# DeltaNet and a maxout layer on one core: loads asked for in the opening, two masks on GpSimd, inverse copies placed elsewhere, the last output's two stores exchanged

## The chip, the cores and the metric

The kernel runs on one core of one Trainium2 chip. The metric is the device time of one execution in microseconds (us). The engines are named as the profile names them: PE (TensorE, matrix products and transposes), DVE (VectorE), ACT (ScalarE), POOL (GpSimd) and SP (SyncE, which here only issues DMAs). Each engine works through its own list of instructions in order; an instruction that waits holds up everything behind it on its engine. An engine that issues a DMA only starts a transfer; the data land later.

## The reference, cut to what matters

For 4 batches and 8 heads, a state of 48 by 48 is carried along 768 positions, and each position reads it and then corrects it. The result, laid out as 3072 rows of 384, goes through a layer that takes the largest of three products.

```python
k_n = k / (norm(k) + 1e-06)
for t in range(S):
    y[t] = q[t] @ state
    v_old = k_n[t] @ state
    state = state + beta[t] * outer(k_n[t], v[t] - v_old)
x = y.transpose(0, 2, 1, 3).reshape(B * S, H * D)
h = maximum(maximum(x @ w1, x @ w2), x @ w3)
out = h @ w_out
```

w1, w2 and w3 are 384 by 768, w_out is 768 by 384, and all four arrive as 64-bit floats.

## The kernel before, in words

**Chunks.** The 768 positions are cut into 12 chunks of 64 (counter c). Within a chunk the positions depend on each other through a triangular matrix of 64 by 64 per head, which is inverted; then a chunk is a handful of matrix products. Two batches lie side by side on the 128 partitions. Keys and queries are loaded as 24 units (two per chunk), turned on PE (`turn`, line 342, copied out at line 348) and multiplied with each other (`gram`, line 419). A product of keys with keys is called `at`, one of keys with queries `pt`. `pt` must be multiplied with a triangular mask before it is used (`masked`, line 403).

**Inverse.** Chunks are inverted two at a time (`solve`). The first call, `solve(0)`, works on blocks of 16 in 15 steps; each step is one DVE multiplication (line 571, tmp from x_bl and y_bl) and one DVE subtraction (line 575, y_bl from y_bl and tmp), all of it in SBUF. Then the block is transposed (line 583), and its parts are copied by `placed` (line 509) into ut0 (chunk 0) and ut1 (chunk 1), four copies for each. `halves_t`, `halves_z`, `halves_u`, `join_z` and `join_u` join blocks of 16 into 32 and 64: DVE transposes (lines 655 and 657), products p_e (line 695), p_f (706), p_z (723), p_j (736), and copies out of PSUM between them (lines 698, 710, 727, 738). `negated_of` chooses the PSUM tiles and the engines for the copies with changed sign (lines 710 and 738). Then `new` makes p_u (line 781, copied out to u at 786), `to_y` makes p_y (823, copied to y at 827) and `to_x` transposes y into xt (842, 849). The chunks 2 and 3 are inverted by `solve(1)`, whose input comes by way of DRAM: `gram` sends `at` out in stores of 32 KB (line 449, 16 of them on SP), and `blocks(1)` fetches all of it back in another order (line 496, on POOL).

**Weights.** `fetch` (line 224) asks for one of 24 pieces of 384 KB into one of five buffers (w_bits). `weights` turns a piece into 32-bit floats in three ACT instructions (lines 251 to 253); one piece later, `joined` adds a DVE shift (line 263) and a POOL integer addition (line 267). Pieces 0, 1 and 2 are the first 128 columns of w1, w2 and w3, and the products p_h (line 1235) of the first columns wait for them.

**Order.** Everything is written out by hand in the order in which each engine is to do it. The opening runs from `load_k(4)` to the loop over `ffn(0)`. From then on, products of the layer are interleaved with the chunks by tables. In the opening the SP queue asks for keys, the queries of units 0 and 1, three weight pieces and the first values, and then makes the 16 stores of `at`. POOL asks for the queries of units 2 and 3. Queries have three places (`qpad[n % 3]`), so unit 3 overwrites unit 0, once that has been turned. POOL also asks for the weight pieces 3, 4 and 5 and the second values (`load_v(1)`) after the first inverse. The queries of units 4, 5 and 6 are asked for by SP in the first three rounds of `ffn(0)`. The masks of units 0 and 1 are made by DVE between the joins; those of 2 and 3 later, in `ffn(0)`. `scale` (line 300, POOL) multiplies the values with the norms of the keys.

**End.** The last three groups of 512 rows use a scheme of seven products (`outputs`; products at line 995, sums by DVE at line 1024, stores at line 1016). The last product of all goes into m5, which is stored by SP and ACT, after m7 has been stored by SP alone.

Of the kernel before, what the change touches and what calls it, by code (L numbers as in the profile page):

```python
# [9 lines left out]
FP32 = mybir.dt.float32  # L10
# [13 lines left out]
def kernel(  # L24
# [82 lines left out]
    def zeros(*tiles):  # L107
        for t in tiles:
            nc.gpsimd.memset(t, 0.0)
# [16 lines left out]
    def load(src, dst, n, queues):  # L126
        c, g = divmod(n, 2)
        for bb in range(2):
            queues[bb].dma_start(
                out=dst[rows(bb ^ g), :, 0:D],  # L130
                in_=src[2 * bb + g, :, c * C : (c + 1) * C, :].rearrange(
                    "h p d -> p h d"
                ),
            )

    def place(n):
        return n % NK if n < 12 else n % 4

    def load_k(n, queues=one_queue):
        load(k, kpad[place(n)], n, queues)  # L140

    def load_q(n, queues=one_queue):
        load(q, qpad[n % NQ], n, queues)

    def load_v(c, queue=nc.sync):
        vts[c] = work.tile([128, 2, H, D], FP32, name="v_t", bufs=3)
# [179 lines left out]
    def turn(n, parts=(0, 1), copy=nc.scalar.copy):  # L326

        if n not in kqts:
            if n == 6:
                kqts[n] = work.tile([128, KT, TOK], FP32, name="xt").rearrange(  # L330
                    "p k t -> p (k t)"
                )[:, 0 : NP * 4 * C].rearrange(
                    "p (j b i t) -> p j b i t", b=2, i=2, t=C
                )
            else:
                kqts[n] = work.tile([128, NP, 2, 2, C], FP32, name="kqt", bufs=6)
        kqt = kqts[n]
        p_t = ps_two("p_t")
        for i in parts:
            src = (kpad[place(n)], qpad[n % NQ])[i]  # L340
            for j in range(NP):
                nc.tensor.transpose(
                    p_t[:, i, j * 128 : (j + 1) * 128],
                    src[:, 2 * j : 2 * j + 2],
                    ident,
                )
        some = slice(parts[0], parts[-1] + 1)
        copy(  # L348
            kqt.rearrange("p j b i t -> p i (j b) t")[:, some],
            p_t.rearrange("p i (x t) -> p i x t", t=C)[:, some],  # L350
        )
# [319 lines left out]
    def negated_of(c, name, w):  # L671
        if c:
            p_v = ps_two(name)[:, :, 0 : H * w].rearrange("p g (h x) -> p g h x", x=w)
            yield range(H), (p_v, p_v), (nc.scalar.mul,) * 2
            return
        p = [
            ps_two(name)[:, :, 0 : NP * w].rearrange("p g (h x) -> p g h x", x=w)
            for _ in range(3)
        ]
        yield range(NP), (p[0], p[0]), (nc.scalar.mul,) * 2  # L680
        yield range(NP, H), (p[1], p[2]), (nc.scalar.mul, nc.vector.tensor_scalar_mul)

    def span(hs):
        return slice(hs[0], hs[-1] + 1)
# [294 lines left out]
    def outputs(m, hs):  # L979
# [9 lines left out]
            a.append(xt[:, t, lo : lo + 256])  # L989
        p, q = (ps_ffn([128, 2, HALF], "p_o") for _ in range(2))  # L990

        def times(to, a, b, start=True, stop=True):
            for g in range(2):
                for j in range(len(a)):
                    nc.tensor.matmul(  # L995
                        to[:, g], a[j][:, 128 * g : 128 * (g + 1)], b[j],
                        start=(start and g == j == 0),
                        stop=(stop and g == 1 and j == len(a) - 1),
                    )

        def x_times(to, lo, right, start=False, stop=True):
            times(
                to,
                [xt[:, KT - 1, lo : lo + 256]],
                [w_sb[0][:, KT - 1, HALF * right : HALF * (right + 1)]],
                start, stop,
            )

        def held(name, dtype_bufs):
# [90 lines left out]
        store(m6, 0, 1)  # L1100
        op(m5, m5, m7, plus)
        yield
        times(p, a22, w["t4"], True, False)
        yield
        x_times(p, 256, 0)
# [2 lines left out]
        yield  # L1108
        x_times(q, 256, 1, True)
        op(m5, m5, q, plus)  # L1110
        store(m5, 1, 1, both_queues)
        yield

    thirds, x_sums = {}, {}

    def cross_hidden(i):

# [17 lines left out]
    def crossed_hidden(m, hs):  # L1135

        banks = upper_pool("banks")
        xt, vec = xts[m], nc.vector.tensor_tensor  # L1140
        plus = vec if m == GROUPS - 1 else nc.gpsimd.tensor_tensor
        lo, hi = slice(0, 256), slice(256, 512)
# [153 lines left out]

    conv = weights()
    solving = solve(0)
    zeros(*(t[:, :, :, D:DP] for t in kmore), qall[:, :, :, D:DP])
    for t in (*ut, st):  # L1300
        nc.vector.memset(t, 0.0)
    warm = small("warm", 1)
# [35 lines left out]
    to_blocks(3, (V, A, V, P))  # L1338
    first_blocks()
    load_q(2, (nc.gpsimd, nc.gpsimd))  # L1340
    turn(4, (0,))
    turn(5, (0,))
    some(solving, 1)
    keys(4)
    keys(5)
    turn(6, (0,))
    turn(0, (1,))
    load_q(3, (nc.gpsimd, nc.gpsimd))
    load_beta()
    keys(6)  # L1350
    gram(0, (1,), None, later=True)
    turn(7, (0,))
    turn(1, (1,))
    keys(7)
    turn(2, (1,))
    gram(1, (1,), None, later=True)
    turn(3, (1,))
    some(conv, 1)
# [1 line left out]
    gram(3, (1,), None, later=True)  # L1360
    some(solving, HB + 1)
    halves_t(0)
    halves_z(0)
    first_norms()
    some(conv, 1)
    placed(1, 0)
    scale(0, nrm_0[:, 0])
    placed(1, 1, nc.gpsimd.tensor_copy)
    blocks(1, nc.gpsimd)
    for _ in range(2):  # L1370
        fetch(nc.gpsimd)
    halves_u(0)
    turn_t1(0)
    join_z(0)
    masked(pts[0], by_par(pts[0]))
    placed(1, 2)
    join_u(0)
    masked(pts[1], by_par(pts[1]))
    old_k(0)
    old_q(0)  # L1380
    new(0)
    some(conv, 1)
    fetch(nc.gpsimd)
    load_v(1, nc.gpsimd)
    placed(1, 3)
    to_y(0)
    busy(2, ident)
    halves_t(1)
# [89 lines left out]
    for i, _ in enumerate(ffn(0)):  # L1478
        if i < 7:
            fetch(nc.sync if i else nc.gpsimd)  # L1480
        if i == 0:
            scale(1, nrm_0[:, 1])
        if i == 1:
            load_q(4)
            load_q(5)
        if i == 2:
            load_q(6)
        for _ in range(FETCHED.get(i, 0)):
            fetch(nc.gpsimd)
        queries(FIRST.get(i, ""))  # L1490
        links(1, EARLY_LINKS.get(i, ""))
        if i == 26:
            solving = solve(2)
            some(solving, 1)
        if i in CONVERTED:
            some(conv, 1)
        if i == 0:
            fetch(nc.gpsimd)
        some(solving, SOLVED.get(i, 0))
        if i in (8, 13):  # L1500
            prep_values(i // 4)
        if i in (4, 8):
            for n in range(2):
                load_k(8 + 2 * (i > 4) + n, (nc.gpsimd, nc.gpsimd))
        if i == 11:
            load_q(11, (nc.gpsimd, nc.gpsimd))
        if i in (3, 9, 10, 21):
            load_v((3, 9, 10, 21).index(i) + 2)
        if i == 18:
            blocks(2)  # L1510
        if i == 30:
            prep_values(4)
        if i in (29, 30, 31):
            load_blocks(i - 17, nc.sync)
        if i in LESS:
            less_first(LESS[i], nc.gpsimd if i < 10 else nc.vector)
        if i in (30, 31):
            turn_first((2 * i - 60, 2 * i - 59))
        if i == 31:
            turn_first((4, 5))  # L1520
            for t in range(KT):
                both_layers(t)
                if t == 0:
                    links(1, "x1")
# [53 lines left out]
```

## Time and profile before

| what | value |
|---|---|
| median of the three runs shown | 503.44 us (501.3, 503.44, 503.69) |
| the profiled execution | 501.88 us, of which the span is 500.1 us |
| busy, share of the span | PE 96%, PEld 69%, DVE 71%, ACT 34%, POOL 38% |
| mean granted TensorE clock | 0.97 |
| DMA | 53.51 MB, mean 107 GB/s |

Cut by stages, the trace gives these busy times in us, and the granted clock and the busy share of the DMA engines beside them:

| stretch, us | PE | DVE | ACT | POOL | clock | DMA share | GB/s |
|---|---|---|---|---|---|---|---|
| 12 to 26 | 9.87 | 11.99 | 7.32 | 6.49 | 0.66 | 1.15 | 198 |
| 26 to 45 | 15.69 | 15.98 | 14.70 | 8.74 | 0.53 | 0.40 | 102 |
| 45 to 65 | 16.34 | 18.37 | 12.94 | 9.08 | 1.00 | 0.92 | 205 |
| 65 to 100 | 34.73 | 29.17 | 24.79 | 27.65 | 1.00 | 0.89 | 181 |

A busy PE is not a PE at its peak, since matrix products are pipelined and their ends are modelled. The chain of waits, followed back from the last instruction, is the view that says what set the end; a stage's row says only which engines had little room in it.

### The profile page before, as it was taken

What the parts mean: (1) busy time and instruction counts of PE and PEld (TensorE: products, weight loads), DVE (VectorE), ACT (ScalarE), POOL (GpSimd) and SP (SyncE); (2) the same over time, 40 slices, a digit from 0 to 9 for tenths busy, and PEclk for the clock granted to TensorE, in tenths of its full rate; (3) what the DMA queues carried; (4) which work ended last, traced back from release to release, by engine and by line L of the source; (5) the groups of instructions that cost most, each with busy time, mean ns of one, the idle gap of its engine ahead of it and who ended that gap; (6) DMA issues with size and microseconds to landing.
All of it is one profiled execution on the core that took longest, in us unless ns stands there. A gap on an engine that the chain in (4) does not pass through costs nothing.

```text
span 500.1 us, 18762 instructions
## 1 busy us (share of the span) xinstructions
PE 480.0 (96%) x8100; PEld 343.7 (69%) x8100; DVE 353.0 (71%) x829; ACT 168.3 (34%) x323; POOL 189.4 (38%) x313
## 2 busy tenths in 40 slices
PE   7779799999999999999999999999999999999996
PEld 6668678878665555565555565565797457998896
DVE  5888999658697352979552998565998864468753
ACT  5576675985330152200243100252211032213210
POOL 7425596764670394780585870601000020000000
PEclk9657999999999999999999999999999999999999
DMA  8936989873351655544775552833223230330002
GB/s 113 196 64 203 200 171 170 199 208 90 81 144 30 138 122 107 145 130 92 147 138 128 137 135 66 171 54 93 65 68 85 55 72 19 86 91 0 1 16 49
DMA packets 110083, 53.51 MB, mean 107 GB/s; under 512 B 93233, under 2 KB 103889, under 8 KB 110001
## 3 DMA queue, kind: packets, MB, share of 16 engines
q1 hardware_dynamic: 98368, 31.91, 31.7%
q0 software_dynamic: 9088, 19.72, 15.8%
q8 instruction: 64, 1.05, 0.9%
q10 hardware_dynamic: 2544, 0.69, 0.8%
q14 instruction: 19, 0.15, 0.1%
HBM read 39.17 MB, written 13.11 MB: 105 GB/s over the span
## 4 chain that ended last, share of the span: by engine, by line
PE 85%; DMA 6%; ACT 3%; POOL 2%; issue 1%; SPq 1%; DVE 1%; POOLq 0%; ACTq 0%; DVEq 0%
PE p_h L1235 32%; PE p_o L1278 13%; PE p_o L995 13%; PE p_c L1173 5%; PE p_g L419 4%; PE p_u L781 2%; PE p_m L915 2%; PE p_y L823 2%; PE p_k L753 2%; DMA kmore<-in_k_dram 2%; PE p_q L753 2%; PE p_s L804 2%; PE p_j L736 2%; PE p_z L723 1%; DMA qall<-in_q_dram 1%
## 5 line engine op out<-in xcount | busy, mean ns | idle before, releaser
L1235 PE MATMUL p_h<-xt,w_sb 128*128 128x512 f32 (+1 forms) x468 | 176.6, 520 | 1.2 <-POOL w_sb L267 0.8
L1235 PEld LDWEIGHTS p_h<-xt,w_sb 128*128 128x128 f32 x468 | 84.5, 190 | 62.4 <-issue 52.8
L1249 DVE TENSOR_TENSOR h<-h,p_h 128x512 f32<-128x512 f32 (+1 forms) x42 | 23.9, 569 | 54.1 <-PE p_h L1235 51.6
L575 DVE TENSOR_TENSOR y_bl<-y_bl,tmp 128x31 f32<-128x31 f32 (+20 forms) x139 | 50.3, 362 | 4.8
L1278 PE MATMUL p_o<-wo_sb,h 128*128 128x384 f32 x144 | 49.2, 490 | 0.4 <-POOL wo_sb L267 0.4
L571 DVE TENSOR_TENSOR tmp<-x_bl,y_bl 128x31 f32<-128x31 f32 (+20 forms) x139 | 45.9, 331 | 4.1
L377 POOL DMA_DIRECT2D turned<-in_q_dram x72 | 39.1, 551 | 5.5 <-POOL turned L372 2.6
L1245 ACT ACTIVATE h<-p_h 128x512 f32<-128x512 f32 (+1 forms) x30 | 16.6, 552 | 70.6 <-PE p_h L1235 70.5
L1278 PEld LDWEIGHTS p_o<-wo_sb,h 128*128 128x128 f32 x144 | 26.8, 190 | 18.5 <-POOL wo_sb L267 1.0
L267 POOL TENSOR_TENSOR w_sb<-mant,up 128x384 int32<-128x384 int32 x18 | 18.7, 1044 | 34.7 <-DVE mant L263 23.7
L419 PEld LDWEIGHTS p_g<-kqt 48*64 48x64 f32 x1216 | 25.1, 145 | 9.8 <-issue 7.6
L419 PE MATMUL p_g<-kqt 48*64 48x64 f32 (+1 forms) x1216 | 28.5, 245 | 0.9 <-ACT kqt L348 0.8
L1284 ACT COPY o_sb<-p_o 128x384 f32<-128x384 f32 x12 | 5.8, 479 | 61.7 <-PE p_o L1278 54.4
L372 POOL MEMSET turned<- 128x96 f32 x18 | 3.3, 190 | 59.2 <-DVE kqt L393 59.2
L608 POOL DMA_DIRECT2D ut<-y_d x4 | 2.6, 650 | 60.4 <-DMA y_d<-y_bl 60.4
L148 POOL DMA_DIRECT2D v_t<-in_v_dram x14 | 11.6, 830 | 28.7 <-PE p_u L781 28.7
L811 DVE TENSOR_TENSOR st<-st,p_s 48x768 f32<-48x768 f32 (+1 forms) x18 | 17.1, 950 | 7.5 <-PE p_s L804 7.1
L403 DVE TENSOR_TENSOR pt<-p_g,mask 128x512 f32<-128x512 f32 x20 | 13.7, 690 | 10.4 <-PE p_g L419 10.3
L1278 PE MATMUL p_o<-w_sb,xt 128*128 128x384 f32 x60 | 21.0, 486 | 0.0
L765 DVE TENSOR_TENSOR v_t<-v_t,p_k 128x768 f32<-128x768 f32 x11 | 10.5, 950 | 13.8 <-PE p_k L753 13.3
L436 ACT COPY at<-p_g 128x512 f32<-128x512 f32 x22 | 12.8, 585 | 18.5 <-DVE pt L403 16.4
L781 PEld LDWEIGHTS p_u<-v_t,ut 64*64 64x64 f32 x768 | 13.7, 141 | 7.2 <-issue 6.1
(240 smaller groups left out, 916.5 us busy)
## 6 DMA issues: line engine op xcount, KB each, us to landing
w_bits<-in_moe_w_dram SPq DMA_DIRECT2D x9, 384.0 KB, 6.7
w_bits<-in_moe_w_dram POOLq DMA_DIRECT2D x9, 384.0 KB, 4.9
turned<-in_q_dram POOLq DMA_DIRECT2D x72, 48.0 KB, 2.6
out_dram<-o_sb SPq DMA_DIRECT2D x36, 96.0 KB, 2.3
y_x<-y SPq DMA_DIRECT2D x32, 96.0 KB, 2.4
qall<-y_x SPq DMA_DIRECT2D x32, 96.0 KB, 2.8
v_t<-in_v_dram POOLq DMA_DIRECT2D x14, 192.0 KB, 4.4
at_d<-at SPq DMA_DIRECT2D x76, 32.0 KB, 2.5
```

The source lines that it names most:

```text
L267: nc.gpsimd.tensor_tensor(out=dst.bitcast(I32), in0=mant_v.bitcast(I32), in1=up_v, op=ALU.add)
L377: (queue, nc.gpsimd)[i].dma_start(out=t[p0 : p0 + 32, bb, at : at + NP * 2 * D].rearrange("p (j x) -> p j x", j=NP), in_=(k, q)[i][2 * bb ...
L419: nc.tensor.matmul(p_g[rows(bb ^ (g * i)), par, c0 : c0 + C * (1 + whole)], kq[:, 0], kq if whole else kq[:, i],)
L571: nc.vector.tensor_tensor(out=t_v, in0=row.to_broadcast(t_v.shape), in1=column.to_broadcast(t_v.shape), op=ALU.mult,)
L575: nc.vector.tensor_tensor(out=rest, in0=rest, in1=t_v, op=ALU.subtract)
L753: nc.tensor.matmul(p_b[rows(bb), par, c0 : c0 + D], kqt[g][dims(par), j, bb ^ g, i], st[dims(par), bb ^ g, g, j],)
L781: nc.tensor.matmul(p_v[rows(bb ^ g), g, i], ut[c % NU][rows(bb), g, h], rhs[rows(bb), g, h],)
L995: nc.tensor.matmul(to[:, g], a[j][:, 128 * g : 128 * (g + 1)], b[j], start=(start and g == j == 0), stop=(stop and g == 1 and j == len(a) ...
L1173: nc.tensor.matmul(to, w[stays], moves, start=(n == 0), stop=(n == len(terms) - 1))
L1235: nc.tensor.matmul(p_h, w_sb[i][:, t, f * 128 : (f + 1) * 128], xt[:, t, lo : lo + w], start=(t == 0), stop=(t == KT - 1),)
L1249: nc.vector.tensor_tensor(out=h, in0=h, in1=p_h, op=ALU.max)
L1278: nc.tensor.matmul(p_o, stays, moves, start=(n == 0), stop=(n == len(terms) - 1))
```

## The change

Nothing is computed otherwise; what changes is who does a step, when it is asked for, and into which place it goes.

1. Unit 3's queries get a place of their own (`third_q`, a buffer of the tile that later holds xt), whose edge POOL clears with one more memset. Their load is issued on POOL right behind unit 2's, ahead of the clearing of y_bl.
2. SP asks for the weight pieces 3, 4 and 5 between the stores of `at`, and then for the queries of units 4, 5 and 6, all in the opening. The three `fetch` calls on POOL and the three loads in `ffn(0)` go.
3. The masks of units 0 and 1 go from DVE to POOL, ahead of `halves_z(0)`, and `load_v(1)` stands on POOL behind them.
4. The copies of the second chunk's inverse: part 0 goes behind `join_u(0)`, part 2 behind the weight piece, part 3 from DVE to POOL (there behind piece 1's addition).
5. `negated_of(0)`: before, the first four heads were copied by ACT alone and the last four by ACT and DVE; after, both halves are shared by ACT and DVE, the second half out of one PSUM tile.
6. In the last group, the product into m7 is computed in two halves, the first ahead of m5's last product and the second behind it in a PSUM bank of its own, and each half is added and stored by itself, on SP and ACT. In the two groups before it, m5 is stored by SP alone.

```diff
+    third_q = work.tile([128, KT, TOK], FP32, name="xt").rearrange(
+        "p k t -> p (k t)"
+    )[:, 0 : H * DP].rearrange("p (h d) -> p h d", d=DP)
+    def q_place(n):
+        return third_q if n == 3 else qpad[n % NQ]
...
-        yield range(NP), (p[0], p[0]), (nc.scalar.mul,) * 2
-        yield range(NP, H), (p[1], p[2]), (nc.scalar.mul, nc.vector.tensor_scalar_mul)
+        by_two = nc.scalar.mul, nc.vector.tensor_scalar_mul
+        yield range(NP), (p[0], p[1]), by_two
+        yield range(NP, H), (p[2], p[2]), by_two
...
+        if m == GROUPS - 1:
+            for g in range(2):
+                if g:
+                    p = last_banks[0].tile(
+                        [128, TOK], FP32, name="p_c", tag="one", bufs=6
+                    )[:, 0:DM].rearrange("p (g x) -> p g x", g=2)
+                times(p, a22, w["t4"], True, False, (g,))
+                x_times(p, 256, 0, False, True, (g,))
+                if g == 0:
+                    x_times(q, 256, 1, True)
+                    op(m5, m5, q, plus)
+                    store(m5, 1, 1, both_queues)
+                op(m7[:, g], m7[:, g], p[:, g], plus)
+                for n in range(2):
+                    s0 = (2 * m + 1) * C
+                    both_queues[n].dma_start(
+                        out=out.rearrange("(b s) d -> b s d", s=S)[
+                            2 * n + g, s0 : s0 + C, 0:HALF
+                        ],
+                        in_=m7[rows(n), g],
+                    )
+            return
...
     load_q(2, (nc.gpsimd, nc.gpsimd))
+    load_q(3, (nc.gpsimd, nc.gpsimd))
...
     keys(5)
+    fetch(nc.sync)
     turn(6, (0,))
     turn(0, (1,))
-    load_q(3, (nc.gpsimd, nc.gpsimd))
     load_beta()
     keys(6)
+    fetch(nc.sync)
...
     keys(7)
+    fetch(nc.sync)
     turn(2, (1,))
+    for n in range(4, 7):
+        load_q(n)
...
     halves_t(0)
+    for n in range(2):
+        masked(pts[n], by_par(pts[n]), nc.gpsimd)
+    load_v(1, nc.gpsimd)
     halves_z(0)
     first_norms()
     some(conv, 1)
-    placed(1, 0)
     scale(0, nrm_0[:, 0])
     placed(1, 1, nc.gpsimd.tensor_copy)
     blocks(1, nc.gpsimd)
-    for _ in range(2):
-        fetch(nc.gpsimd)
     halves_u(0)
     turn_t1(0)
     join_z(0)
-    masked(pts[0], by_par(pts[0]))
-    placed(1, 2)
     join_u(0)
-    masked(pts[1], by_par(pts[1]))
+    placed(1, 0)
     old_k(0)
     old_q(0)
     new(0)
     some(conv, 1)
-    fetch(nc.gpsimd)
-    load_v(1, nc.gpsimd)
-    placed(1, 3)
+    placed(1, 2)
+    placed(1, 3, nc.gpsimd.tensor_copy)
     to_y(0)
...
-        if i == 1:
-            load_q(4)
-            load_q(5)
-        if i == 2:
-            load_q(6)
```

## The prediction

> **What bounds it now.** I read the page first, then the chain of waits in order of time, then the timeline of each engine in the stretches that the change touches. The chain is PE for 85% of the span; from 64.8 us on it hardly leaves PE. So nearly all that this change can give or take lies ahead of 64.8 us, where PE waits, and in the last microseconds.
>
> ```profile
> 26.37 2.00 DVE L583 STREAM_TRANSPOSE x_bl<-y_bl 128x1024 f32<-128x1024 f32 x1
> ...
> 30.86 0.71 DVE L655 STREAM_TRANSPOSE t<-ut 128x512 f32<-128x512 f32 x1 [0.84 <-ACT ut L509]
> ...
> 37.30 1.54 DVE L403 TENSOR_TENSOR pt<-pt,mask 128x512 f32<-128x512 f32 x1
> ...
> 39.49 0.42 DVE L738 TENSOR_SCALAR ut<-p_j 32x256 f32<-32x256 f32 x1
> ```
> ```profile
> 24.88 0.59 ACT L430 COPY pt<-p_g 128x512 f32<-128x512 f32 x1 [0.51 <-PE p_g L419]
> ...
> 28.71 1.04 ACT L430 COPY pt<-p_g 128x512 f32<-128x512 f32 x2
> 29.78 1.70 ACT L509 COPY ut<-x_bl 32x512 f32<-32x512 f32 x2
> ```
>
> These are the timelines of DVE and ACT (start, duration, idle time before in brackets). solve(0) ends with the transpose at 28.37, but ACT copies the masks' sources out of PSUM until 29.75 and starts its share of the copies only at 29.78: 1.4 us in which DVE could be late at no cost. Then everything alternates: copies, p_f, copies, p_j, copies, p_u. At 37.30 DVE makes mask 0 and holds up its copy of p_j, which ends at 39.91; the second half of p_u waits for that.
>
> ```profile
> 42.11 1.32 POOL w_sb L267
> ...
> 50.13 0.27 DVE mant L263
> ...
> 54.65 7.25 DMA w_bits<-in_moe_w_dram
> ...
> 61.98 0.57 ACT mant L251
> ...
> 64.82 0.78 PE p_u L781 x34
> ```
>
> In the chain (start, duration) the second half is DVE's list: halves_t(1) at 43.48, the prologue of solve(1), piece 2's shift at 50.05, POOL's addition until 51.54, and then p_h at 51.60; then a weight piece that takes 7.25 us to land and keeps ACT idle for 1.20 us until 61.98.
>
> **Part 1, masks on POOL.** Two masks leave DVE (1.54 and 0.69) and come on POOL. POOL's multiplication of 128x768 takes 1.49 and its 128x384 takes 1.01 (line 892), so 128x512 is an estimated 1.17. Where do they fall? Mask 0 follows the four beta issues, which end at 21.16, less the 1.35 of the two query issues that move ahead: 19.8 to 21.0. Mask 1's source is ready at 25.47 (the ACT fence). Both fall inside the recurrence of solve(0), DVE operations with two inputs in SBUF. What such a meeting costs is shown later, at the same lines 571 and 575:
>
> ```profile
> 134.71 0.25 DVE L571 TENSOR_TENSOR tmp<-x_bl,y_bl 128x87 f32<-128x87 f32 x1
> 135.00 2.25 DVE L575 TENSOR_TENSOR y_bl<-y_bl,tmp 128x87 f32<-128x87 f32 x1
> ```
> ```profile
> 134.00 1.63 POOL L377 DMA_DIRECT2D turned<-in_q_dram  x3
> 135.64 1.49 POOL L300 TENSOR_TENSOR v_t<-v_t,nrm 128x768 f32<-128x768 f32 x1
> ```
>
> The first fence is DVE, the second POOL: the subtraction takes 2.25 instead of 0.25 and ends 0.12 after POOL's multiplication does. At 289.22 it is 2.35 instead of 0.40. Both times POOL's instruction stood behind DMA issues, and the loss was its duration plus 0.5. Without issues ahead, an operation at 123.20 lost 0.70 to an addition of 0.99 that it met 0.15 after its start. Operations that read PSUM, and the transposes, kept their durations beside POOL. So mask 0 (behind four issues) costs 1.17 + 0.5 = 1.67, mask 1 some 1.1: **2.75**. Bounds: 0 and 4.0 (both like line 300); no DVE work leaves this stretch, so a gain is excluded.
>
> The Trainium skill (SBUF — State Buffer, section "SBUF: two separate sides") calls the port pair that the two engines share "an exclusive lock, not a bandwidth split", held for the whole instruction, the other starting some 115 ns after its end. By that rule the two masks would cost 2 x (1.17 + 0.12) = 2.55, since it has no 0.5 ahead of an instruction; the rows here show it, and decide.
>
> **Part 2, followed down the alternation.** solve(0) ends 2.75 late and its transpose at 31.12. The 1.4 of slack takes half. ACT copies from 31.15 (before 29.78: +1.37); halves_t(0) follows DVE's own copies (1.62) and ends at 34.95 (before 33.04: +1.9). p_f runs 35.0 to 37.0. Here `negated_of` helps: ACT and DVE take two copies each (0.6) behind p_f, to 37.65, where ACT alone needed until 36.16 (+1.5). DVE's transposes (1.35) end at 39.0 (+1.7), p_j (1.4) at 40.4, and its last copy, now free of mask and placed copy, at 40.87: only **+0.96**. So part 5 and the freed DVE give back 0.8. But p_u no longer waits between its halves; begun at 40.25, it takes its 2.1 to 42.35 (before 40.95: +1.4), and u, p_y and y follow, y at 44.85 (before 43.45).
>
> **Part 3, the last placed copy.** halves_t(1) reads all of ut1. Before, its last part was DVE's copy (until 42.57), under p_y's cover. Now it is POOL's, behind piece 1's addition, which waits for DVE's shift behind u: 43.45 + 1.32 + 1.02 (line 509 on POOL at 37.26) = 45.8. That is 1.0 after y, so halves_t(1) starts at 45.85 instead of 43.48: **+2.4**. If POOL's addition takes 0.99, it is 2.05. The prologue of solve(1), piece 2's addition and p_h at 51.60 follow, all +2.4: DVE is busy there without a gap.
>
> **Part 4, the loads.** Unit 3's queries took 7.29 and kept turn(3) waiting 0.86; that goes, but only makes ACT's copies ready earlier than DVE, which is now later: 0. The first memset and the masks on POOL stand in 13.4 us of idle time there: 0 beyond the above. Between 45 and 65 us the DMA engines are 0.92 busy at 205 GB/s, between 26 and 45 only 0.40 at 102. Six query loads (96 KB each), piece 5 and the second values move from the full stretch to the other. So piece 7, still issued by POOL, meets 192 KB less of unit 6 beside it, about 1.0 us at that rate, and most of ACT's wait of 1.20 goes. PE's own list (p_q and p_h, ending 64.14) then releases p_u 0.68 earlier than 64.82. I take **-0.65**; bounds 0 and -1.2.
>
> On SP three pieces now stand between the stores. An issue took 0.63 to 3.56. Before, the last store was issued at 32.3, and POOL asked for all of them back at 38.24; after, POOL reaches that at 39.9, so up to 5 us of lateness is covered. Conversions aren't started earlier: pieces 3 to 5 wait for buffers that the additions free.
>
> **Part 6, the end.** PE's last five products (0.81) now belong to m7's second half. m5's sum ends at 495.2, its stores are issued on both queues until 495.85, m7's first two until 496.5, the last two start there. Before, the last issue started at 496.73 and landed 2.4 later:
>
> ```profile
> 495.39 1.25 SPq L1016 DMA_DIRECT2D out_dram<-o_sb  x2
> 496.73 0.59 SPq L1016 DMA_DIRECT2D out_dram<-up  x1
> ```
>
> **-0.2**; bounds -0.5 (smaller stores land sooner) and +0.2 (ACT's store took 2.8).
>
> **Sum**: 2.4 - 0.65 - 0.2 = +1.55. From 64.8 us on PE waits little, so the shift stays. The profiled execution took 501.88 (span 500.1 and 1.8 around it), which gives 503.4; it lies 1.56 below the median shown, 503.44, on which I put the forecast: **505.0**.
>
> **Rivals.**
> *The masks don't delay the recurrence* (its operations are short, POOL might slip between them). Then ACT starts at 28.9 by the query's 0.86, p_f ends 0.8 earlier, the last p_j copy at 38.27 (-1.6), and p_u, no longer waiting, at 39.75 (-1.2); POOL's late copy lets halves_t(1) start at 43.25 (-0.2). With -0.65 and -0.2: -1.1, 502.4. At the good ends (copy hidden -1.2, all of the DMA wait -1.2, -0.5) it is -2.9, 500.5. For it: POOL's addition at 50.55 beside the recurrence of solve(1) cost nothing, but there y_p lies in PSUM. Against it: the two rows above.
> *The stores come too late* (slower). Stores of the last unit wait behind pieces 3 and 4 on SP; POOL's fetch of solve(1)'s input waits for them, and piece 1's addition and the placed copy are queued behind that on POOL, and the square root, the zeroing of y_p and both copies into xt behind its landing on ACT. It decides when the stores have landed only after 42.3, when the addition (43.45) comes late, 2.4 us or more after 39.9; two issues at 3.56 each and a landing of 7.2 instead of the stores' 2.3 would put it at 42 to 45. It adds 1.5 to 3: about 507.0. Against it: at 27 to 33 us the DMA engines have room.
> *The change in PSUM tiles or the new place of unit 3 adds a wait.* The new place is free, its successor xt comes 18 us later, and p_f's second tile waits for the copy whose result it needs anyway: nothing, so it has no time of its own.
>
> **Chances.** Forecast (504.0 to 506.5) 0.50, of which 0.38 within 0.5% and 0.12 above; no delay by masks 0.28, of which 0.15 within and 0.13 faster; late stores 0.22, slower. A difference of 0.5% (2.5 us) is about what a measurement of this kernel can tell from no change. So faster 0.13, same 0.53, slower 0.34. The range takes in the first rival's good end and the second's middle with the bound of the masks (1.25 more than I took): 500.5 to 507.5; the forecast's own is 504.0 to 506.5.
>
> **What would show it.** In the profile after: lines 571 and 575 of solve(0) with two operations of over 1.2 us, and its transpose at about 29 instead of 26.4; both masks on POOL inside it; p_u's halves without a gap; halves_t(1) at about 45.9, behind POOL's copy; the p_h that waits for piece 2 at about 54; no wait of ACT for piece 7; the last store landing 2.2 to 2.8 after its issue. If the recurrence keeps its durations, the first rival holds; if POOL waits ahead of line 496, the second.

## The result, and the profile after

The changed kernel takes 506.20 us (median of 17 runs, 502.91 to 509.22), the kernel before 503.03 us (17 runs on the same chip, 500.64 to 506.56). The ratio is 1.0063, with a 95% interval of 1.0034 to 1.0091: slower by 1.7 to 4.6 us. All ratios here come from executions in the faster of two states that the kernel shows, so they are not quite the quotients of the medians. The profiled execution of the changed kernel took 506.74 us, with a span of 505.0 us, so 4.9 us more than the span of before. The profiled execution of before lies 1.15 us under its median, that of after 0.54 us above its own; a comparison of the two profiles therefore shows some 1.7 us more than the medians do.

In the changed kernel most line numbers are 7 or 8 higher (571 is 578, 583 is 590, 655 is 662, 723 is 731, 781 is 789), those of the layer's products 31 (1235 is 1266).

The masks first, in the timelines of DVE and of POOL after the change (start, duration, engine, line, tiles; idle time before in brackets):

```profile
19.83 1.47 DVE L578 TENSOR_TENSOR tmp<-x_bl,y_bl 128x110 f32<-128x110 f32 x1
21.34 0.27 DVE L582 TENSOR_TENSOR y_bl<-y_bl,tmp 128x110 f32<-128x110 f32 x1
...
25.49 1.25 DVE L578 TENSOR_TENSOR tmp<-x_bl,y_bl 128x96 f32<-128x96 f32 x1
26.78 0.26 DVE L582 TENSOR_TENSOR y_bl<-y_bl,tmp 128x96 f32<-128x96 f32 x1
```
```profile
19.89 1.28 POOL L410 TENSOR_TENSOR pt<-pt,mask 128x512 f32<-128x512 f32 x1
25.36 1.27 POOL L410 TENSOR_TENSOR pt<-pt,mask 128x512 f32<-128x512 f32 x1 [4.19 <-ACT pt L437]
```

Each mask falls into the recurrence of solve(0), and the one DVE step that meets it takes 1.47 and 1.25 us instead of 0.27 and 0.26. The transpose behind the recurrence starts at 28.61 instead of 26.37.

What the prediction did not have shows in PE's timeline. The first view is before the change, the second after it:

```profile
35.62 1.23 PE L723 MATMUL p_z<-ut,at 32*32 32x32 f32 x64 [0.47 <-ACT ut L710]
36.81 1.81 PE L736 MATMUL p_j<-z,t 32*32 32x32 f32 x64
38.85 2.10 PE L781 MATMUL p_u<-v_t,ut 64*64 64x48 f32 x62 [0.23 <-issue]
```
```profile
36.32 0.57 PE L731 MATMUL p_z<-ut,at 32*32 32x32 f32 x25
38.51 0.78 PE L731 MATMUL p_z<-ut,at 32*32 32x32 f32 x39 [1.61 <-issue]
39.36 1.79 PE L744 MATMUL p_j<-z,t 32*32 32x32 f32 x64
41.08 0.89 PE L789 MATMUL p_u<-v_t,ut 64*64 64x48 f32 x22
44.03 1.21 PE L789 MATMUL p_u<-v_t,ut 64*64 64x48 f32 x36 [2.07 <-issue]
```

The 64 products of p_z are torn after the 25th, those of p_u after the 22nd, and in both gaps PE waits for nothing that the profile names ("issue"). Together they are 3.68 us. Then DVE's timeline, down to halves_t(1):

```profile
45.58 0.56 DVE L794 COPY u<-p_u 128x384 f32<-128x384 f32 x1 [2.92 <-PE p_u L789]
...
47.37 0.56 DVE L835 COPY y<-p_y 128x384 f32<-128x384 f32 x1 [0.32 <-PE p_y L831]
49.09 0.71 DVE L662 STREAM_TRANSPOSE t<-ut 128x512 f32<-128x512 f32 x1 [1.16 <-POOL ut L516]
```

u waits 2.92 us for the torn p_u, and halves_t(1) then waits 1.16 us for the copy that POOL makes behind its addition. It starts at 49.09 instead of 43.48. The p_h that waits for piece 2 comes at 57.22 instead of 51.60, the first p_u of chunk 1 at 69.77 instead of 64.82, and the last product ends at 501.24 instead of 495.42. Behind that the end has become shorter (SP's timeline):

```profile
497.96 2.87 SPq L1024 DMA_DIRECT2D out_dram<-up  x3
500.93 1.22 SPq L1126 DMA_DIRECT2D out_dram<-o_sb  x2
```

From the end of the last product to the end of the span it takes 3.79 us instead of 4.69.

### The profile page after: what moved, and what is told of

Its sections match the earlier page's. It is cut to its first block, busy times and chain, and to the rows that moved or that the text cites. A ratio compares the mean times of both kernels' runs of the same rounds, so it can differ in the third digit from the quotient of the medians.

```text
span 505.0 us, 18768 instructions
## 1 busy us (share of the span) xinstructions
PE 480.5 (95%) x8100; PEld 344.3 (68%) x8100; DVE 355.7 (70%) x830; ACT 167.2 (33%) x320; POOL 190.6 (38%) x314
## 4 chain that ended last, share of the span: by engine, by line
PE 80%; DVE 9%; DMA 3%; issue 2%; POOL 2%; SPq 1%; ACT 1%; ACTq 0%; POOLq 0%; DVEq 0%
PE p_h L1266 29%; PE p_o L1309 13%; PE p_o L1003 12%; PE p_c L1204 5%; PE p_g L426 4%; PE p_m L923 2%; PE p_u L789 2%; PE p_k L761 2%; DVE tmp L578 2%; PE p_y L831 2%; PE p_q L761 2%; PE p_j L744 2%; PE p_z L731 1%; PE p_s L812 1%; PE p_e L1204 1%
## 5 line engine op out<-in xcount | busy, mean ns | idle before, releaser
L578 DVE TENSOR_TENSOR tmp<-x_bl,y_bl 128x31 f32<-128x31 f32 (+20 forms) x139 | 52.7, 379 | 4.1
L582 DVE TENSOR_TENSOR y_bl<-y_bl,tmp 128x31 f32<-128x31 f32 (+20 forms) x139 | 48.2, 347 | 4.8
```

The lines of the kernel that those rows point to most:

```text
L578: nc.vector.tensor_tensor(out=t_v, in0=row.to_broadcast(t_v.shape), in1=column.to_broadcast(t_v.shape), op=ALU.mult,)
L582: nc.vector.tensor_tensor(out=rest, in0=rest, in1=t_v, op=ALU.subtract)
```

## What the gaps on PE are

The records of the DMA packets in the trace have a queue of their own for instructions. This is the list of queues of the changed kernel between 30 and 46 us (packets, MB, share of the 16 engines):

```profile
q1 hardware_dynamic: 7084, 2.10, 63.0%
q0 software_dynamic: 170, 0.56, 12.0%
q8 instruction: 3, 0.05, 1.3%
```

The packets of q8 have 16 KB each. The fourth and fifth of an execution stand against PE's two gaps like this (us; the order is the same in all kernels; the stops are PE's longest waits for "issue" in p_z and p_u):

| kernel | 4th packet starts, has landed | PE stops in p_z, goes on | 5th packet starts, has landed | PE stops in p_u, goes on |
|---|---|---|---|---|
| before | 32.59, 33.87 | 0.3 at most | 36.95, 37.83 | 0.2 |
| after | 35.97, 36.98 | 36.90, 38.51 | 41.23, 42.35 | 41.97, 44.03 |
| q_late (below) | 34.38, 35.43 | 36.86, 37.03 | 39.07, 40.04 | 41.12, 41.36 |
| p13_dve (below) | 34.42, 35.51 | 0.3 | 39.48, 40.70 | 40.96, 42.15 |

In the changed kernel the packets come 3.4 and 4.3 us later than before, while PE itself is only 0.7 and 2.2 us later at these places, and PE goes on 1.5 and 1.7 us after the landing. This holds wherever such a gap is found: between 28 and 480 us, the fourteen profiles of this study have 26 gaps of PE of 0.6 us or more that are put to issue (none of them in before, all in p_z, p_j, p_u, p_k and p_s), and each of the 26 ends 1.28 to 1.82 us after a packet of q8 has landed. Packets come mostly 4 to 7 us apart between 30 and 75 us, so this is no coincidence. The gaps also stand at the same few places of PE's list in all kernels, to within two products (in chunk 0 always after the 25th product of p_z and the 22nd of p_u), and two neighbouring places lie 125 to 127 products apart, with as many weight loads between them. The profile of each kernel has 64 packets of q8 for 8100 products and 8100 weight loads, 253 instructions to a packet. So PE had run out of instructions at the end of a block. The Trainium skill ("Runtime: NRT & Kernel Launch", section "Instruction fetch mechanics") says that instructions are fetched in blocks of 16 KiB, 256 at a time, while the engine works, and that the cost of crossing from one to the next is "mostly hidden". The size agrees with the packets here; that it is hidden does not hold in this stage: 1.61 and 2.07 us. The products here are short (64 of p_z in 1.23 us): before the change, PE came from the place in p_z to the one in p_u, 125 products, in 3.5 us.

What delays the packets can be read only indirectly. Measured from PE's own progress, the fourth packet has landed 1.6 to 2.1 us after PE starts its 471st product in the eight profiles whose weight pieces are asked for as before, and 2.3 to 4.1 us after it in the six with the pieces in the opening (4.1 in the changed kernel). These are PE's rows of three stretches, before and after (stretch and its length, PE's busy time and instructions, granted clock, share of the DMA engines, GB/s):

```profile
34.00:39.00 5.00, 4.21 (x174) 0.50 0.02 4
39.00:45.00 6.00, 5.90 (x140) 0.59 0.67 227
45.00:52.00 7.00, 5.58 (x142) 1.00 0.87 208
```
```profile
34.00:39.00 5.00, 3.33 (x129) 0.50 0.78 195
39.00:45.00 6.00, 3.68 (x145) 0.50 0.71 163
45.00:52.00 7.00, 6.68 (x102) 0.67 0.02 4
```

The first fence is before, the second after. Where PE runs through its shortest products, the DMA engines moved 4 GB/s before and move 195 GB/s after. The moved loads took a stretch in which the DMA engines were all but idle (0.02), and that was the stretch in which PE needs its instructions fastest.

## The experiments

Theory A: the loads asked for in the opening delay PE's instruction packets, and these gaps make most of the loss. The rivals are the two other causes that the profile shows: the masks' hold on the recurrence, and the copy on POOL ahead of halves_t(1). The kernel before was measured beside each group of four: 505.33 us in the first (29 runs), 504.93 in the second and 505.56 in the third (35 runs each). Each ratio is against the kernel before of its own group.

### First group

**loads_late**: the changed kernel with the loads put back, the masks left on POOL.

```diff
     keys(5)
-    fetch(nc.sync)
...
-    for n in range(4, 7):
-        load_q(n)
...
     blocks(1, nc.gpsimd)
+    for _ in range(2):
+        fetch(nc.gpsimd)
...
+    fetch(nc.gpsimd)
+    load_v(1, nc.gpsimd)
     placed(1, 2)
     placed(1, 3, nc.gpsimd.tensor_copy)
```

> The kernel after, with pieces 3 to 5, the second values and the queries of units 4 to 6 asked for where the kernel before asks for them; masks stay on POOL. Theory A (the two gaps of PE in p_z and p_u, 1.6 and 2.1 us in the profile after, are PE's own instructions arriving late behind the early loads): no such gap over 0.6 us, the transpose of solve(0) still ends at about 30.5 us, the first p_u of chunk 1 starts at 66 to 67 us instead of 69.8, and the time is 0 to 1.5 us above the kernel before. Theory B (the gaps are chance, and the masks alone make the loss): gaps appear or not without regard to the loads, and the time is about that of the kernel after, 3 us above.

Measured: 509.68 us, ratio 1.0111 (1.0057 to 1.0164). The gaps in p_z and p_u are gone, as theory A wants, but the time is longer. POOL's copy now stands behind the issues of the weight piece and of the values (46.45 to 48.12), so it starts only at 48.16, and halves_t(1) waits for it 3.5 us. A placed copy on POOL costs whatever POOL has in front of it.

**masks_dve**: the changed kernel with both masks on DVE, between the joins; the early loads stay.

```diff
-    for n in range(2):
-        masked(pts[n], by_par(pts[n]), nc.gpsimd)
     join_z(0)
+    masked(pts[0], by_par(pts[0]))
     join_u(0)
+    masked(pts[1], by_par(pts[1]))
```

> The kernel after, with both masks back on DVE between the joins; the loads stay early. Theory A: the transpose of solve(0) ends at about 28.4 us, but PE still has gaps of over 1 us in all in p_z, p_j, p_u or nearby that nothing in the profile ends, and the time is 0 to 2 us above the kernel before. Theory B: no loss is left, and with the gain at the end the time is 1 to 2 us below the kernel before.

Measured: 508.05 us, 1.0054 (1.0016 to 1.0092). The recurrence is free of long steps and its transpose is back at 26.39. But here, in an execution of 511.12 us, 3.1 above the median, the prediction's second rival comes true: POOL waits 4.68 us for the stores before it can fetch the input of solve(1) at 43.63, and ACT's root waits for that fetch (ACT's timeline):

```profile
49.49 0.26 ACT L281 ACTIVATE root_bl<-wo_sb 128x32 f32<-128x32 f32 x1 [5.19 <-DMA wo_sb<-at_d]
```

The copies into xt stand behind the root on ACT, and p_h waits 4.31 us for them. In the changed kernel itself the same fetch was issued at 39.51, after a wait of 0.61, and the root did not wait: the early loads leave this little room, and the execution shown here used it up.

**both_back**: loads and masks both as before; unit 3's place, the other copies and the end stay changed.

```diff
     join_z(0)
+    masked(pts[0], by_par(pts[0]))
     join_u(0)
+    masked(pts[1], by_par(pts[1]))
...
+    fetch(nc.gpsimd)
+    load_v(1, nc.gpsimd)
     placed(1, 2)
     placed(1, 3, nc.gpsimd.tensor_copy)
```

> The kernel after with both the loads and the masks as in the kernel before; what stays is unit 3's place and early load, the placed copies, the shared copies of p_f and p_j, and the end. Theory A and B: transpose of solve(0) at 28.4 us or earlier, no gap in p_z and p_u, and the time 1 to 2 us below the kernel before (0.9 of it at the end).

Measured: 508.33 us, 1.0069 (1.0032 to 1.0106). Up to y nothing has moved (42.88; before 42.89). Then DVE waits for POOL:

```profile
42.88 0.56 DVE L835 COPY y<-p_y 128x384 f32<-128x384 f32 x1
47.15 0.71 DVE L662 STREAM_TRANSPOSE t<-ut 128x512 f32<-128x512 f32 x1 [3.71 <-POOL ut L516]
```

As in loads_late, issues of 2.4 us stand between POOL's addition and its copy. The p_h of piece 2 comes 3.7 us later than before.

**extra_loads**: the kernel before, with six more loads of 96 KB on SP behind the stores, which nothing reads.

```diff
     turn(2, (1,))
+    for n in range(4, 7):
+        load(q, unread, n, one_queue)
```

> The kernel before, with six more loads of 96 KB on SP behind the stores of at, into a place that nobody reads. Nothing waits for them but SP's own queue. Theory A: PE gets gaps of 1 us or more in p_z, p_j, p_u or nearby that nothing in the profile ends, and the time is 1 to 3 us above the kernel before. Theory B: no such gaps, and the time is within 0.5 us of the kernel before, unless a later load lands late.

Measured: 506.33 us, 1.0043 (1.0011 to 1.0075). More traffic alone costs time. Yet the gaps are not in p_z and p_u: they are in p_k (0.89 at 54.35) and p_j (1.43 at 60.70), ending 1.32 and 1.52 us after a packet of q8. The DMA engines are fuller there (1.12 and 1.07 busy from 52 to 58 and 58 to 65 us, where before had 0.85 and 1.03), but masks_only (below) has gaps at the same two places (0.89 and 0.88) without these loads, so that they made the gaps is not shown.

### Second group

**p13_dve**: the changed kernel with part 3 of the second chunk's inverse on DVE.

```diff
-    placed(1, 3, nc.gpsimd.tensor_copy)
+    placed(1, 3)
```

> The changed kernel, only with part 3 of the second chunk's inverse copied by DVE again. Theory P (the copy on POOL is part of the loss): DVE copies at once behind u or under p_y, the wait of 1.16 us ahead of halves_t(1) goes, halves_t(1) starts 0.9 to 1.2 us earlier against y than in the changed kernel, and the p_h that waits for piece 2 comes about 1 us earlier (56.2 instead of 57.2); time about 1 us under the changed kernel, ratio to before about 1.004. Theory A (PE's late instruction loads make most of the loss): the gaps in p_z and p_u stay, 3 to 4 us together, wherever halves_t(1) stands. Rival: the addition of piece 1 on POOL sets the end in place of the copy, and nothing changes (ratio 1.006).

Measured: 507.54 us, 1.0048 (1.0018 to 1.0078). The wait of 1.16 us ahead of halves_t(1) is gone; but DVE's two copies together take 1.92 instead of 1.2, since the second (45.17 to 46.48) is held by POOL's addition (44.70 to 46.02). The gap in p_u stays (1.20), that in p_z has shrunk to 0.3. halves_t(1) starts 2.0 us earlier than in the changed kernel, but the two gaps are 2.2 us shorter, so the copy's return to DVE by itself gained nothing here.

**q_late**: the changed kernel with the queries of units 4 to 6 asked for in ffn(0) again; weight pieces and masks stay.

```diff
-    for n in range(4, 7):
-        load_q(n)
+        if i == 1:
+            load_q(4)
+            load_q(5)
+        if i == 2:
+            load_q(6)
```

> The changed kernel, only with the queries of units 4, 5 and 6 asked for in the rounds of ffn(0) again; the weight pieces 3 to 5 stay on SP between the stores, and the masks on POOL. Theory A1 (the six query loads behind the stores, 0.6 MB, fill the DMA engines from 36 to 45 us and starve PE's instruction loads): the gaps in p_z and p_u shrink from 3.7 to under 1 us together, y comes about 44.5 instead of 47.4, and the time is some 2 us under the changed kernel (ratio to before about 1.002), less what piece 7 then waits again (0.7). Theory A2 (the weight pieces, 1.2 MB, do it): the gaps stay at 2 us or more, and the ratio stays at 1.005 to 1.008.

Measured: 506.61 us, 1.0049 (1.0022 to 1.0076). PE's timeline:

```profile
36.29 0.57 PE L731 MATMUL p_z<-ut,at 32*32 32x32 f32 x25
37.03 1.28 PE L731 MATMUL p_z<-ut,at 32*32 32x32 f32 x39 [0.17 <-issue]
...
40.15 0.97 PE L789 MATMUL p_u<-v_t,ut 64*64 64x48 f32 x22
41.36 1.51 PE L789 MATMUL p_u<-v_t,ut 64*64 64x48 f32 x42 [0.24 <-issue]
```

The 3.68 us have become 0.41, and p_u's second half comes 2.67 us earlier: in this execution the weight pieces alone hardly tear PE's list. How much of the rest is the queries' is not shown, since p13_dve, with the same loads as the changed kernel, had gaps of 1.51 us there. The first p_u of chunk 1 is 1.97 us earlier than in the changed kernel (67.80). The measured time falls by less than the intervals can tell apart. This execution lost another 3.9 us against before between 70 and 495 us, two thirds of it around 256 us, where p_z has a gap of 1.17 us of the same kind.

**masks_only**: the kernel before with the two masks on POOL ahead of `halves_z(0)`.

```diff
     halves_t(0)
+    for n in range(2):
+        masked(pts[n], by_par(pts[n]), nc.gpsimd)
     halves_z(0)
...
     join_z(0)
-    masked(pts[0], by_par(pts[0]))
```

> The kernel before, only with the masks of units 0 and 1 made by GpSimd ahead of halves_z(0); loads, copies and the end as before. Theory L (each mask holds up one recurrence step of solve(0) for about its own 1.27 us): two of the 30 steps take 1.2 to 1.5 us, the transpose ends about 2.1 later (30.5), of which ACT's copies ahead cover 1.4, and DVE without its masks (1.5 and 0.7 in the joins) gives the rest back: p_u within 0.5 us of before, time within 0.7 us of before (ratio 0.999 to 1.0015). Rival: the lateness is passed on whole, +2.1 us (ratio 1.004). Other rival: with the loads where they were, POOL takes the masks later and outside the recurrence, the transpose is not later, and the time is some 1 us under before (ratio 0.998).

Measured: 506.53 us, 1.0052 (1.0024 to 1.0080). Its timeline of DVE:

```profile
20.18 1.31 DVE L575 TENSOR_TENSOR y_bl<-y_bl,tmp 128x110 f32<-128x110 f32 x1
21.52 2.45 DVE L571 TENSOR_TENSOR tmp<-x_bl,y_bl 128x120 f32<-128x120 f32 x1
```

POOL made both masks here back to back from 21.27 to 23.83, so one step is held through both, and the step before it already waits from 20.18, beside the last beta issues. The transpose is 3.3 us later than before, p_x 2.3 and the p_h of piece 2 2.7: the lateness is passed on, and DVE's freed time gives little of it back. This execution (510.48 us) lies 4 us above the median.

**back_p13**: both_back, with part 3 on DVE too.

```diff
     placed(1, 2)
-    placed(1, 3, nc.gpsimd.tensor_copy)
+    placed(1, 3)
```

> As both_back (loads and masks as before), and part 3 of the second chunk's inverse on DVE too; what is left of the change: unit 3's own place and earlier load, the parts 0 and 2 copied later, the negated copies shared by two engines, and the exchanged end. Theory P: halves_t(1) starts at 43.5 or earlier (both_back 47.15), the p_h that waits for piece 2 within 0.5 us of before (51.6), and the time is 0 to 1.5 us under before (ratio 0.997 to 1.000), the end giving at most 0.9. Rival: the late copies of parts 0 and 2 on DVE, ahead of u or halves_t(1), take the place of the wait: halves_t(1) 0.7 to 1.5 later than 43.5, ratio 1.002.

Measured: 505.48 us, 1.0020 (0.9991 to 1.0050). halves_t(1) is back at 43.80 and the p_h of piece 2 at 51.87 (before 51.60). Against both_back that is 3.4 us at this p_h. This shows the copy on POOL as a cause by itself where DMA issues stand in front of it, as they do in both_back; in the changed kernel none do, and there p13_dve shows no gain.

### Third group

**loads_only**: the kernel before with the loads of the change and nothing else of it.

```diff
     keys(5)
+    fetch(nc.sync)
...
     turn(2, (1,))
+    for n in range(4, 7):
+        load_q(n)
...
     halves_t(0)
+    load_v(1, nc.gpsimd)
     halves_z(0)
```

> The kernel before, with nothing of the change but its loads: unit 3's own place, three weight pieces and the queries of units 4 to 6 on SP in the opening, the second values early on POOL; masks, copies and end as before. Theory A (the early loads starve PE's instruction loads): gaps of 1 to 2 us in which PE waits for nothing that the profile shows stand in p_z, p_j or p_u between 34 and 45 us, y is 2 to 3.5 us late, and the ratio is 1.004 to 1.008. Prediction's view (the early loads fall where the DMA engines have room and only relieve piece 7, -0.65): no such gap, ratio 0.997 to 1.000. Third view, late stores: POOL's fetch of the second inverse's input waits 2 us or more and ACT's copies into xt wait for that, ratio 1.005 or more without gaps on PE.

Measured: 507.72 us, 1.0043 (1.0006 to 1.0080). Theory A fails here: between 28 and 75 us there is no gap of 0.6 us (one of 0.82 stands in p_z at 260 us). In this execution the first step of the recurrence came at 20.65 instead of 17.70 (a chance of the opening: masks_behind, whose opening is that of ends_kept, had it too, 20.57 against 17.99), and PE met the traffic later (p_z at 38.03 instead of 35.62). What came late instead is the fetch for solve(1), behind a weight piece:

```profile
42.21 0.61 POOL L503 DMA_DIRECT2D wo_sb<-at_d  x1 [1.51 <-DMA w_bits<-in_moe_w_dram]
```

ACT's root waited 3.0 us for it, and p_h 2.70 us for ACT. So in the profiles the early loads cost time in this way or in the other.

**q_late_p13**: the changed kernel without the early queries and with part 3 on DVE.

```diff
-    for n in range(4, 7):
-        load_q(n)
...
-    placed(1, 3, nc.gpsimd.tensor_copy)
+    placed(1, 3)
```

> The changed kernel with the queries of units 4 to 6 back in the rounds of ffn(0) and part 3 of the second chunk's inverse on DVE: the two suspects taken away together; the masks on POOL, the weight pieces on SP and the exchanged end stay. If the two together make the loss: no gap of 1 us in p_z, p_j, p_u; the p_h that waits for piece 2 at 52 to 53.5 (changed kernel 57.2), ratio 0.999 to 1.002. If the masks' hold on the recurrence (+2.1 at the transpose) makes most of it: the p_h at 54 or later, ratio 1.004 to 1.006.

Measured: 506.79 us, 1.0021 (0.9988 to 1.0054). There is no gap of 0.6 us between 28 and 75 us (one of 1.54 stands in p_z at 258 us), and the p_h of piece 2 comes at 54.73 (changed kernel 57.22). Of the +3.1 us that are left there, the masks in the recurrence make most: two of its steps took 2.05 and 1.23 us, and the transpose came 3.2 us later, 0.4 of it from a later start of the recurrence.

**ends_kept**: the kernel before, with only unit 3's place, the shared negated copies and the new end.

```diff
     load_q(2, (nc.gpsimd, nc.gpsimd))
+    load_q(3, (nc.gpsimd, nc.gpsimd))
...
-        yield range(NP), (p[0], p[0]), (nc.scalar.mul,) * 2
-        yield range(NP, H), (p[1], p[2]), (nc.scalar.mul, nc.vector.tensor_scalar_mul)
+        by_two = nc.scalar.mul, nc.vector.tensor_scalar_mul
+        yield range(NP), (p[0], p[1]), by_two
+        yield range(NP, H), (p[2], p[2]), by_two
...
+        if m == GROUPS - 1:
```

> The kernel before with what is left when the loads of weights, values and late queries, the masks and all copies of the second inverse are as before: unit 3's own place and earlier load, the negated copies shared, and the exchanged end. Theory E (the end gives 0.9, the shared copies up to 0.7 in the opening, nothing else acts): the last matmul 0 to 0.7 us earlier, span behind it 3.7 instead of 4.7, time 1 to 1.6 us under before, ratio 0.997 to 0.998. Rival (the gain of the opening is eaten at the weight piece that lands at 61.9, and only the end counts): ratio 0.998. Other rival (the order of the later transfers makes it as slow as back_p13): ratio 1.002.

Measured: 506.90 us, 1.0039 (1.0011 to 1.0067). Expected was a gain. Up to the p_h of piece 2 it is 0.2 us ahead of before, and behind the last product it takes 3.63 us instead of 4.69. In between it loses:

```profile
54.38 1.01 PE L761 MATMUL p_k<-st,kqt 48*64 48x48 f32 x54
57.12 0.47 PE L761 MATMUL p_k<-st,kqt 48*64 48x48 f32 x10 [1.73 <-issue]
```

There is a gap in p_k, where before has none, and one of 1.08 in p_z at 256.71, after which the granted clock of the stretch 256 to 262 is 0.73 (before 1.00, with a gap of 0.3). Nothing of the edit acts at these places, and the packets were late there as elsewhere (the one for p_k landed at 55.81; PE went on at 57.12).

**masks_behind**: ends_kept, with both masks on POOL behind part 1's copy, after the recurrence.

```diff
     placed(1, 1, nc.gpsimd.tensor_copy)
+    for n in range(2):
+        masked(pts[n], by_par(pts[n]), nc.gpsimd)
```

> As ends_kept, with both masks on GpSimd, yet behind the second chunk's part 1, after the recurrence, where DVE reads PSUM or transposes. Theory L (only the recurrence's operations with two inputs in SBUF are held up by a GpSimd multiplication): steps of the recurrence keep 0.2 to 0.3 us, the transpose stays at 26.4, DVE loses its 1.5 and 0.7 us of masks, y comes about 1 us earlier than in ends_kept; ratio 0.996 to 0.997. Rival: the masks (1.27 each) put the fetch for the second inverse and piece 1's addition 2.5 us later on POOL, and what waits for them (halves_t(1)'s neighbours, copies into xt) eats more than that: ratio 1.000 to 1.004.

Measured: 509.95 us, 1.0069 (1.0032 to 1.0107). The recurrence takes 8.67 us from its first step to its transpose, as before (8.67): masks outside it do not hold it. But they take POOL's time ahead of the fetch for solve(1), which is issued at 42.85 (37.12 in ends_kept, whose recurrence began 2.6 us earlier); ACT's root waits 2.1 us for it and p_h 2.0. In this execution p_k also had a gap of 3.89 us, ending 1.81 after a late packet.

None of the twelve is faster than the kernel before; two, back_p13 and q_late_p13, can't be told from it.

## Why the prediction was wrong where it was

The forecast was 505.0 us, with a difference too small to measure as the likeliest (0.53; slower had 0.34); measured were 506.2 us and a difference of 0.63%. The time lies inside the range, 1.2 us above the forecast. That is in part luck: the sum gave +1.55 us, the medians differ by 3.17 and the profiles by 4.9, and a loss of 3.68 us that the sum lacks was partly made up by masks that cost less and an end that gave more than forecast.

- **Masks.** The step holds: both fell inside the recurrence, and DVE was held until 0.14 and 0.11 us after POOL's instruction had ended. Its size: 1.20 + 0.99 = 2.19 us in the changed kernel instead of 2.75, since the 0.5 ahead of the first mask was not there. The Trainium skill's rule (SBUF — State Buffer, section "SBUF: two separate sides") gave 2.55, closer in this execution, though its lag of some 115 ns is stated there for a DMA of GpSimd behind VectorE. Other executions show the time ahead as well (loads_late 2.05 + 1.35, q_late_p13 2.05 + 1.23 in two steps of 0.26 to 0.29 each: losses of 2.85 and 2.74 by the recurrence's whole length).
- **The alternation.** p_f started 0.8 us late and ended 1.2 late (forecast 1.9 for both). halves_t(1) is 5.61 us late, of which 1.16 are its wait for POOL; without the two gaps of PE, DVE would have been through y 4.45 - 3.68 = 0.77 us late (forecast 1.4). So, by subtraction, the arithmetic through the copies, the shared negated copies and p_u's joined halves was right within 0.7 us, and 0.56 of that is the masks'.
- **The step that failed** is part 4: "Six query loads (96 KB each), piece 5 and the second values move from the full stretch to the other", with "bounds 0 and -1.2". The stretch with room was taken to be free, so that the loads could only gain; a loss was left out of the bounds without a reason. They were costed only by what waits for DMAs that the kernel itself issues. PE's instructions come by DMA packets too, and the trace of before has them in its records (one from 36.95 to 37.83, p_u begins at 38.85). The loads were laid exactly there, for +3.68 us in the profiled execution.
- **The last placed copy.** The wait behind y was forecast as 1.0 and measured as 1.16. back_p13 against both_back confirms the mechanism, but in p13_dve the copy on DVE cost about as much: POOL's addition then held up DVE's copy ahead of y.
- **The weight piece.** ACT's wait for piece 7 fell from 1.20 to 0.49 us, and of the 5.61 us at halves_t(1) 4.95 are left at the first p_u of chunk 1: -0.66, forecast -0.65.
- **The end.** It was given 0.2 and gave 0.90 (4.69 to 3.79). All ten kernels with the new end take 3.63 to 3.81 us behind the last product, the four with the old one 4.69 to 5.01. What was mis-sized is how much the smaller stores and the earlier issue give: the last product ends at 501.24, the last issue starts 0.62 us later instead of 1.31 (forecast 1.1), and all issues are through by 502.41.
- **Sum in the profiles.** 0.77 + 1.16 = 1.93 at halves_t(1) by the forecast's own terms (forecast 2.4), + 3.68 of gaps, - 0.66, + 0.87 that gathers between 65 and 495 us, - 0.90: 4.92, the difference of the spans.
- **Rivals.** "The masks don't delay" is refuted. "The stores come too late" was not what happened in the profiled execution of the changed kernel (POOL waited 0.61), but it happened in masks_dve and loads_only, at the upper end of the price that was put on it or above (forecast 1.5 to 3; p_h waited 4.3 and 2.7 us).

**What stays open.** That PE stops for late packets rests on the times and places of 26 gaps. That other data make the packets late rests on the fourth packet, which landed late in all six profiles with the early weight pieces and in none of the other eight; the trace does not tell on which DMA engine a packet ran. Whether PE then stops differs from execution to execution: in p_z and p_u of chunk 0 the changed kernel lost 3.68 us, p13_dve 1.51, q_late 0.41 and loads_only nothing. Such gaps are not the early loads' alone either: all six kernels with the loads as before and some other part of the change have one or more of 0.67 to 3.89 us at 50 us or later. The parts do not add up either: masks alone cost 0.52%, loads alone 0.43%, the rest 0.39%, all together 0.63%, with intervals of about 0.3% each. Why ends_kept is slower, with a better opening and a better end, isn't settled: its profile puts the loss into gaps of PE's instructions at 55 and 256 us, but the one profile of before (501.88 us) is from an execution 3 to 4 us under the medians of the second and third group, so it may just have been spared such gaps.

## What to carry to other kernels

A stretch in which the DMA engines are idle need not be free if an engine runs through many short instructions there: look for the packets of the instruction queue in it, and keep bulk loads off it or place them behind it. Give a copy to another engine only after reading what stands in front of it on that engine's list, DMA issues included. And an operation for GpSimd with its data in SBUF can cost VectorE nearly its whole length, if it falls among VectorE's operations with two inputs in SBUF, however short these are (here 1.20 and 0.99 us for two of 1.28 and 1.27).

## What the runs showed of the hardware

- A PE that has run out of instructions goes on 1.28 to 1.82 us after a 16 KB packet of them has landed (26 of 26 gaps); such packets take 0.9 to 2.3 us.
- A DVE step could be held before the GpSimd multiplication that it met had begun: in loads_late from 19.75, with POOL's last issue from 19.80 and its mask only from 20.38; in masks_only from 20.18, 1.09 us ahead of the mask. Other steps beside the same kind of issue kept their 0.24 to 0.27 us. What decides between the two isn't settled.
- A copy of DVE with its source in SBUF (0.61 us alone) took 1.3 beside POOL's integer addition, in p13_dve and in back_p13 alike.
- After a gap of 1.08 us in p_z, six products of 128x512 took 4.54 us (ends_kept, from 257.98), at a granted clock of 0.73 in the stretch from 256 to 262; before, after a gap of 0.32, the same six took 2.84 at 1.00.
